# Seven-product second product for three token groups, shorter scale and root chains, and a new written-out order

## The chip, the cores and the metric

The kernel runs on one core of a Trainium2 chip. The metric is the device time of one execution in microseconds (us). Three executions of the kernel before took 697.19, 697.19 and 699.59 us, median 697.19 us. The profile that is read below is of one more execution, which took 698.44 us.

## The reference

Three stages follow one another on 2304 tokens (4 batches of 576). The matrices are large enough that most of the arithmetic lies in the last stage.

```python
# 1: attention, 8 heads of 64; heads 0-3 see the last 32 positions,
#    heads 4-7 every fourth of the last 128
scores = where(mask[h], q @ k.T / 8, -1e9)
x = softmax(scores) @ v                       # 2304 x 512
# 2: first MLP, d_ff 1024
h = x @ moe_w_in
solu = h * softmax(h)
ln = (solu - mean(solu)) / sqrt(var(solu) + 1e-6) * g_ln
y = ln @ moe_w_out                            # 2304 x 512
# 3: second MLP, d_ff 2048
h = y @ moe2_w_in
g = maximum(h, 0) + log1p(exp(-abs(h)))       # softplus
out = g @ moe2_w_out                          # 2304 x 512
```

Inputs and outputs are float32; the `moe` weights (first MLP and second) arrive as 64-bit floats.

## The kernel before, in words

**Precision.** Almost every product runs in float16 on TensorE (PE). Each operand is scaled by a power of two and split into a high and a low float16 half, and the product is three matmuls that add up in PSUM: high by high, high by low, low by high. A *split* is therefore two instructions per operand: the high half (VectorE, called DVE here, or ScalarE, called ACT), then the low half as a residue (DVE, `scalar_tensor_tensor` or `tensor_tensor`).

**Scales.** For each of the ten weight pieces (`w1i`, `w1o`, four quarters of `w2i` and of `w2o`) and for q, k and v of each batch, ACT squares the pieces and leaves one column of sums per piece. PE multiplies these columns by a matrix of ones (a float32 matmul, line L552), which gives every partition the column totals; DVE then adds the columns (`tensor_reduce`, L738 or L660) and makes the scale out of the sum in four one-column instructions (`scale_of`, L580: floor, two shifts, reciprocal, times a power of two). The weights cannot be split before that.

**Root.** For each of 18 token tiles of 128, the layer norm needs one over the root of the variance. `m1` (L1186) computes it on DVE in one-column instructions: an integer first guess (shift, then subtract from a constant) and three Newton steps of two instructions, then a last multiplication.

**Groups.** The second MLP works on groups of 256 tokens, numbered 0 to 8. Groups 0 to 4 go through `mlp2`: for each of eight blocks of 256 hidden features, the hidden product, softplus on ACT, a split of the result `g`, and the second product (`outp`): for two halves of the tokens and two halves of the features three matmuls of 128x512, so 12 a block. Groups 5, 6 and groups 7, 8 are *twins*: `mlp2_twin` takes two groups at once and does the first product of each feature quarter (a `unit`) in seven half-size products `P1` to `P7` instead of eight (L1550). For that `twin_weights` makes sums and differences of the weights, `y_twin` those of y, and DVE adds up the seven results (`U`, `C`). The second product of the twins is the same `outp` as above, 12 matmuls of 128x512 a block:

```python
for ti in range(2):
    for ff in range(2):
        f = 2 * fh + ff
        for x, (a, w) in enumerate(((0, 0), (0, 1), (1, 0))):
            mm(po.t[:, ti], gb.t[:, a, ff, ti*128:(ti+1)*128], w2o[qd][:, w, f, :], ...)
```

At the end of a group two instructions bring the PSUM accumulators into `osb` and two transfers write 256 rows of the output.

**Order.** Every instruction belongs to a named operation with the operations that it comes after and the buffers that it uses. Nothing is scheduled at run time: the table `ORDER` (L190) lists the operations one by one, `SLOTS` the buffer that each takes, and the engines get their instructions in that order; all transfers are issued by SyncE (SP) in that order too. Negative entries of `ORDER` are *fills*: matmuls of the identity `eye` by itself, 128x512 in bfloat16, into a free PSUM bank, whose result nobody reads. There are 142 of them, all in the first third of the program.

Of the kernel before, what the change touches and what calls it, by code (L numbers as in the profile page):

```python
# [1749 lines left out]
```

## Time and profile before

| | |
|---|---|
| executions, us | 697.19, 697.19, 699.59 (median 697.19) |
| the profiled execution, us | 698.44 |
| its span, first to last instruction, us | 696.5 |
| PE busy, us (share) | 675.2 (97%) |
| DVE busy, us (share) | 556.0 (80%) |
| ACT busy, us (share) | 480.9 (69%) |
| TensorE clock granted, mean | 0.988 of full |
| HBM read, written, MB | 54.53, 4.72 |

The profiled execution lasted 1.9 us longer than its span (698.44 against 696.5), which is what lies before its first and behind its last instruction. "Busy" is the time in which an engine had at least one instruction in flight; a busy PE may also be running fills. The chain of waits is the chain of work that ended last, followed back from the last instruction; 69% of the span on it is PE, 12% DVE and 10% DMA.

### The profile page before, as it was taken

The page shows a single profiled execution, that of the slowest core. Times are in us where ns is not written, and L with a number is a line of the kernel's source. Part 1 is how long each engine was busy: PE and PEld are TensorE (multiplying, and loading weights), DVE is VectorE, ACT ScalarE, POOL GpSimd, SP SyncE. Part 2 cuts the span into 40 slices and gives each one's busy share as a digit, 9 for nine tenths or more (in the row PEclk, how much of TensorE's full clock was granted, in tenths as well). Part 3 has the DMA queues.
Part 4 walks back from the last instruction along what each step waited for, and adds up shares of the span by engine and source line. Part 5 has one row for each costly group of instructions (what it writes and reads, how often), then busy time and mean ns, then how long its engine had stood idle before and what let it go on. Part 6 is the DMA issues. An engine that isn't in the chain of part 4 may idle for free.

```text
span 696.5 us, 14184 instructions
## 1 busy us (share of the span) xinstructions
PE 675.2 (97%) x5223; PEld 463.9 (67%) x5223; DVE 556.0 (80%) x1619; ACT 480.9 (69%) x1015; POOL 3.5 (1%) x22
## 2 busy tenths in 40 slices
PE   7999699999999999999999999999999999999997
PEld 4665547766765588688667668666776668676653
DVE  4999999999999968788889899887887768544233
ACT  4889998999998776987799797976364632322312
POOL 2000000000000000000000000000000000000000
PEclk9999689999999999999999999999999999999999
DMA  9889987669876558989887887652012110000001
GB/s 266 247 233 259 225 225 193 162 170 188 184 147 164 146 176 185 200 162 157 158 152 153 153 162 136 116 113 43 1 31 62 31 31 1 1 32 31 1 1 60
DMA packets 186773, 89.80 MB, mean 129 GB/s; under 512 B 157000, under 2 KB 174416, under 8 KB 186704
## 3 DMA queue, kind: packets, MB, share of 16 engines
q1 hardware_dynamic: 186704, 88.90, 56.4%
q8 instruction: 41, 0.67, 0.4%
q14 instruction: 28, 0.23, 0.1%
HBM read 54.53 MB, written 4.72 MB: 85 GB/s over the span
## 4 chain that ended last, share of the span: by engine, by line
PE 69%; DVE 12%; DMA 10%; ACT 4%; issue 3%; SPq 1%; ACTq 0%; DVEq 0%
PE ps_w L552 31%; PE bank L552 26%; PE bank L1550 11%; DMA xd<-x 2%; DVE E L543 2%; DMA E<-in_v_dram 2%; DMA qT<-qk 1%; DMA pT<-p 1%; DVE W L543 1%; PE bank L558 1%; DVE s L1122 1%; DMA W<-in_moe_w_out_dram 1%; ACT E L534 1%; DMA rv<-in_v_dram 1%; DMA rq<-in_q_dram 1%
## 5 line engine op out<-in xcount | busy, mean ns | idle before, releaser
L552 PE MATMUL ps_w<-W,g 128*128 128x512 f16 x864 | 194.3, 379 | 0.0
L552 PEld LDWEIGHTS <-W 128*128 128x128 f16 x1824 | 176.5, 98 | 23.3 <-DMA lnT<-hl 0.7
L552 PEld LDWEIGHTS <-g 128*128 128x128 f16 x864 | 83.6, 98 | 91.4
L552 PE MATMUL bank<-y,W 128*128 128x256 f16 x960 | 109.9, 273 | 0.0
L552 PE MATMUL ps_w<-W,xr 128*128 128x512 f16 x432 | 99.5, 382 | 1.0 <-ACT xr L534 1.0
L552 PE MATMUL bank<-lnT,W 128*128 128x256 f16 x864 | 98.7, 273 | 0.2 <-DMA lnT<-hl 0.2
L552 PEld LDWEIGHTS <-xr 128*128 128x128 f16 x432 | 42.1, 99 | 46.9 <-ACT xr L534 1.5
L543 DVE SCALAR_TENSOR_TENSOR g<-r,KR,g 128x512 f16<-128x512 f32 x68 | 50.3, 744 | 15.2 <-ACT g L534 14.2
L1718 ACT ACT_TABLE_LOAD x43 | 55.2, 1283 | 0.7
L1550 PEld LDWEIGHTS <-W 128*128 128x128 f16 x480 | 47.0, 98 | 8.4
L534 ACT ACTIVATE E<-E 128x768 f32<-128x768 f32 (+3 forms) x51 | 37.9, 744 | 15.7 <-DVE E L543 8.8
L534 ACT ACTIVATE s<-s 96x128 f32<-96x128 f32 (+3 forms) x144 | 43.5, 374 | 2.4 <-DVE st L538 1.2
L1122 DVE CUSTOM_DVE_ANT_0 s<-bank,band,bsc 96x128 f32<-96x128 f32 (+3 forms) x144 | 38.9, 324 | 3.9 <-PE bank L552 3.6
L534 ACT ACTIVATE r<-bank,invC 128x512 f32<-128x512 f32 x40 | 27.2, 685 | 16.4 <-PE bank L552 15.5
L534 ACT ACTIVATE r<-r,invT 128x512 f32<-128x512 f32 x21 | 14.6, 714 | 32.5 <-DVE r L546 32.4
L534 ACT ACTIVATE xf<-bank,rs 80x64 f32<-80x64 f32 (+1 forms) x128 | 29.3, 314 | 7.2 <-DVE rs L549 4.8
L552 PE MATMUL ps_w<-eye 128*128 128x512 bf16 x108 | 31.4, 407 | 0.7 <-DVE e L543 0.7
L534 ACT ACTIVATE g<-r,KR 128x512 f16<-128x512 f32 x35 | 24.9, 715 | 6.6 <-PE ps_w L552 6.3
L552 PEld LDWEIGHTS <-pT 128*96 128x96 f16 (+3 forms) x432 | 23.1, 123 | 6.9 <-issue 1.5
L543 DVE SCALAR_TENSOR_TENSOR E<-E 128x512 int32<-128x512 int32 x40 | 27.1, 683 | 0.1
L552 PEld LDWEIGHTS <-eye 128*128 128x128 bf16 (+2 forms) x162 | 16.5, 111 | 15.8 <-POOL eye L611 4.0
L534 ACT ACTIVATE hl<-e,st 128x1024 f16<-128x1024 f32 x18 | 22.3, 1242 | 5.4 <-DMA lnT<-hl 3.2
(295 smaller groups left out, 1102.9 us busy)
## 6 DMA issues: line engine op xcount, KB each, us to landing
E<-in_moe_w_in_dram SPq DMA_DIRECT2D x17, 512.0 KB, 4.8
E<-in_moe_w_out_dram SPq DMA_DIRECT2D x17, 512.0 KB, 4.1
out_dram<-osb SPq DMA_DIRECT2D x18, 256.0 KB, 2.4
W<-in_moe_w_in_dram SPq DMA_DIRECT2D x7, 512.0 KB, 5.7
W<-in_moe_w_out_dram SPq DMA_DIRECT2D x7, 512.0 KB, 6.2
E<-in_v_dram SPq DMA_DIRECT2D x9, 384.0 KB, 4.0
E<-in_q_dram SPq DMA_DIRECT2D x9, 384.0 KB, 3.4
E<-in_k_dram SPq DMA_DIRECT2D x9, 384.0 KB, 3.4
```

Source lines behind the costliest of these rows:

```text
L534: pin(nc.scalar.activation(out=out, in_=in_, func=func, **kw))
L543: pin(nc.vector.scalar_tensor_tensor(out=out, in0=in0, scalar=s, in1=in1, op0=op0, op1=op1, **kw))
L552: pin(nc.tensor.matmul(out, l, r, start=start, stop=stop))
L558: pin(nc.tensor.transpose(out, in_, eye32[:in_.shape[0], :in_.shape[0]]))
L1122: pin(nc.vector.tensor_tensor_reduce(out=sv()[:rows, h, :nk], in0=sb.t[:rows, h, :nk], in1=band[:rows, 48 - m:48 - m + nk], scale=sc[:rows ...
L1550: pin(nc.tensor.matmul(ps.t[:, ff, :], at(w, cc, ff), yo.t[:, v, cc, :], start=start, stop=cc == 1 and x == 2, skip_group_check=True,))
L1718: pin(nc.scalar.preload_act_table_set(TABLES[tab]))
```

## The change

**Second product of groups 6, 7 and 8** (`OTW`). The blocks of these three groups are kept back until their `g` is there and then go through `out_seven`: the 256 tokens by 256 features of `g` and the 256 features by 512 columns of the weights are cut into two halves each way, and seven products of quarter matrices replace eight. One block is then 7 products of 3 matmuls of 128x256, so 21 matmuls instead of 12 of 128x512. What DVE and ACT have to do for that:

- `twin_out_weights`, once for each of the eight blocks of weights, shared by the three groups: two sums that rebuild the float32 weight (128x512), four differences (128x256), two splits (128x512).
- in `step`, for each block of each group: the ordinary split, now for 384 of 512 columns; four sums and differences of 128x128 (`so..1`, `.3`, `.2`, `.4`, each on the result of the one before), and a second split, 128x512 (`ho`, `lo`).
- `end`, for each group: eight instructions of 128x256 that scale the seven results and add them up, instead of two of 128x512.

The new buffers lie in memory that the attention, the first MLP and the y stage have left; the third weight sum of `twin_weights` moves into a part of `w2i` itself, behind the last plain hidden product.

**Chains.** The totals are now added up on PE (one float32 matmul per column, all into one PSUM column), the `tensor_reduce` is gone, and the reciprocal and its multiplication have become one integer instruction, so that `scale_of` is three instructions. The root's chain has seven instructions ahead of the last multiplication instead of nine (shift and subtraction in one, two of the Newton steps replaced by one step of higher order).

**Order.** `ORDER` and `SLOTS` are new throughout. The transfers on SP stand in the same order up to the 79th; fills are 132 instead of 142.

```diff
+    OTW = (6, 7, 8)
...
-        65, 66, 247, 248, 278, 277, 0, 13, -2, -2, -2, 250, 252, 2943, 3, 2945, 14, 67, 69, -2, -2, 280, 254, 281,
...
+        63, 231, -2, 234, 232, -2, 236, 3146, 64, 235, -2, -2, 238, 239, 262, 261, 264, 265, 250, 0, 1, 13, 3, 4,
...
-            (TINY, lambda e: ts(sc, ss() if callable(ss) else ss, 2.0 ** -80, op0=ALU.max)),
+            (dve_cost(0, x=1), lambda e: ts(sc, ss(), 2.0 ** -80, op0=ALU.max), [], uses),
             (TINY, lambda e: ts(i, i, 24, 23, ALU.logical_shift_right, ALU.logical_shift_left)),
-            (TINY, lambda e: recip(inv, sc)),
-            (TINY, lambda e: ts(inv, inv, 2.0 ** -50)),
+            (TINY, lambda e: ts(inv.bitcast(INT32), i, -1.0, float((254 - 50) << 23), ALU.mult, ALU.add)),
...
-        m = P.op(f"{name}m", pe_cost(0.15), lambda e: mm(pb.t[:, 0:n], ones, am[:, 0:n], True, True), after=squares, uses=[pb])
+        def total(e):
+            for i in cols:
+                mm(pb.t[:, 0:1], ones, am[:, i:i + 1], i == cols[0], i == cols[-1])
...
-            (TINY, lambda e: pin(nc.vector.tensor_reduce(out=t[:, 0:1], in_=pb.t[:, 0:n], axis=AXX, op=ALU.add)), [], [pb]),
-            *scale_of(inv, sc, t[:, 0:1]),
+            *scale_of(inv, sc, lambda: pb.t[:, 0:1], [pb]),
...
-            lambda e: ts(i32(9), i32(7), 1, op0=ALU.logical_shift_right),
-            lambda e: ts(i32(9), i32(9), -1.0, float(0x5F3759DF - 2 ** 31), ALU.mult, ALU.add),
+            lambda e: ts(i32(9), i32(7), -0.5, float(0x5F3759DF - 2 ** 31), ALU.mult, ALU.add),
             lambda e: stt(col(10), col(9), col(9), col(7), ALU.mult, ALU.mult),
-            lambda e: stt(col(9), col(10), 3.0, col(9), ALU.subtract, ALU.mult),
+            lambda e: stt(col(8), col(10), 10.0 / 3.0, col(10), ALU.subtract, ALU.mult),
+            lambda e: stt(col(9), col(8), 5.0, col(9), ALU.add, ALU.mult),
             lambda e: stt(col(10), col(9), col(9), col(7), ALU.mult, ALU.mult),
-            lambda e: stt(col(9), col(10), 12.0, col(9), ALU.subtract, ALU.mult),
-            lambda e: stt(col(10), col(9), col(9), col(7), ALU.mult, ALU.mult),
-            lambda e: stt(col(10), col(10), 768.0, col(9), ALU.subtract, ALU.mult),
+            lambda e: stt(col(10), col(10), 64.0 / 3.0, col(9), ALU.subtract, ALU.mult),
...
+    def twin_out_weights(p):
...
+            P.op(
+                f"to{p}f{i}", dve_cost(512), lambda e, i=i: tt(F[i].t, wt[:, 0, f + i, :], wt[:, 1, f + i, :], ALU.add),
+                after=[*w2_d[p // 2][1]], uses=[F[i]],
+            ) for i in range(2)
...
+        t1 = P.op(f"to{p}t1", dve_cost(256), lambda e: tt(F[0].t[:, lo], F[0].t[:, hi], F[0].t[:, lo], ALU.subtract), after=[o[0]], uses=[F[0]])
...
+    def out_seven(n):
...
+        def step(p, k, rb, gb, split):
...
+            cost = dve_cost(128)
+            s1 = P.op(f"so{m}.1", cost, lambda e: tt(a22(), a21(), a22(), ALU.add), after=split, uses=[rb])
+            s3 = P.op(f"so{m}.3", cost, lambda e: tt(a21(), a11(), a21(), ALU.subtract), after=[s1], uses=[rb])
+            s2 = P.op(f"so{m}.2", cost, lambda e: tt(a11(), a22(), a11(), ALU.subtract), after=[s3], uses=[rb])
+            s4 = P.op(f"so{m}.4", cost, lambda e: tt(a12(), a12(), a11(), ALU.subtract), after=[s2], uses=[rb])
+            h2 = P.op(f"ho{m}", either(512, ptr=1), lambda e: scaled(e, g2.t[:, 0], rb.t, KR[:, cq]), after=[s4], uses=[rb, g2])
...
+                for q, gt, ff, t, b, start in which:
+                    start = start and new
+                    for x, (a, w) in enumerate(((0, 0), (0, 1), (1, 0))):
+                        pin(nc.tensor.matmul(
+                            mi[q](), gt.t[:, a, ff, 128 - 128 * t:256 - 128 * t], b(w), start=start and x == 0, stop=x == 2, skip_group_check=True,
+                        ))
...
+            parts = {
+                "a": ((1, gb, 0, 0, plain(0, 0), True),),
+                "b": ((5, g2, 1, 1, summed(0), True), (6, g2, 0, 0, summed(3), False), (7, g2, 0, 1, summed(1), True)),
+                "c": ((2, gb, 1, 0, plain(1, 0), False), (4, gb, 1, 1, summed(2), False), (3, g2, 1, 0, plain(1, 1), True)),
+            }
+            ready = {"a": split, "b": [h2, l2], "c": [*split, h2, l2]}
...
+        def end():
...
+            u2 = plus("u2", lambda: ub.t[:, hi], 6, lambda: ub.t[:, lo], [m1_, *all_ops["b"]], [*both, ub])
...
+            c12 = plus("c12", lambda: o1.t[:, hi], 3, lambda: o1.t[:, hi], [u4, *all_ops["c"]], [*both, o1])
+            c21 = plus("c21", lambda: o2.t[:, lo], 4, lambda: o2.t[:, lo], [u3, c22, *all_ops["c"]], [*both, o2], niD[:, 0:1])
```

**The order at two places.** The first is DVE at the scale of the first weight, `w1i` (`s1i` holds that scale, `bank` is PSUM, `W` and `E` hold raw weights, `xr` and `s` belong to the attention). Before:

```order
L1013 TENSOR_REDUCE s_112<-bank_139 96x4
L546 TENSOR_TENSOR xr<-bank_138,xr 128x2x72
L540 TENSOR_SCALAR W<-E 128x512
L738 TENSOR_REDUCE tmp_90<-bank_137 128x1
L538 TENSOR_SCALAR s1i<-tmp_90 128x1
L540 TENSOR_SCALAR s1i<-s1i 128x1
L549 RECIPROCAL s1i<-s1i 128x1
L538 TENSOR_SCALAR s1i<-s1i 128x1
L543 SCALAR_TENSOR_TENSOR W<-E,W 128x512
L538 TENSOR_SCALAR W<-W,s1i 128x512
```

And with the change:

```order
L562 TENSOR_TENSOR xr<-bank_138,xr 128x2x72
L1034 TENSOR_REDUCE s_113<-bank_139 96x4
L556 TENSOR_SCALAR W<-E 128x512
L554 TENSOR_SCALAR s1i<-bank_138 128x1
L556 TENSOR_SCALAR s1i<-s1i 128x1 x2
L559 SCALAR_TENSOR_TENSOR W<-E,W 128x512
L554 TENSOR_SCALAR W<-W,s1i 128x512
```

Five one-column instructions have become three, and the first of them reads PSUM itself. On PE one matmul `bank<-amw,ones 128x8` has become eight of 128x1.

The second place is the end of DVE's program (`g` and `s`, `v` hold splits, `r`, `e` and `W` softplus results, `p` a sum of the last group, `osb` output rows). Before:

```order
L546 TENSOR_TENSOR r_126<-bank_137,osb_135 128x512
L543 SCALAR_TENSOR_TENSOR g_131<-hl,KR,g_131 128x512
L538 TENSOR_SCALAR g_130<-r_126,KR 128x512
L538 TENSOR_SCALAR osb_133<-ps_w_141,iD 128x512
L538 TENSOR_SCALAR g_129<-r_127,KR 128x512
L543 SCALAR_TENSOR_TENSOR g_129<-r_127,KR,g_129 128x512
L543 SCALAR_TENSOR_TENSOR g_130<-r_126,KR,g_130 128x512
L538 TENSOR_SCALAR osb_133<-ps_w_140,iD 128x512
```

And with the change, of which these are 12 consecutive rows shortly before the last sums of `end`:

```order
L562 TENSOR_TENSOR W<-W 128x128 x3
L559 SCALAR_TENSOR_TENSOR s_113<-e_118,KR,s_113 128x512
L559 SCALAR_TENSOR_TENSOR s_114<-W,KR,s_114 128x512
L559 SCALAR_TENSOR_TENSOR g_132<-r_127,KR,g_132 128x384
L562 TENSOR_TENSOR r_127<-r_127 128x128 x2
L559 SCALAR_TENSOR_TENSOR g_131<-r_126,KR,g_131 128x384
L562 TENSOR_TENSOR r_127<-r_127 128x128
L562 TENSOR_TENSOR r_126<-r_126 128x128
L562 TENSOR_TENSOR r_127<-r_127 128x128
L562 TENSOR_TENSOR r_126<-r_126 128x128 x3
L559 SCALAR_TENSOR_TENSOR v_112<-r_127,KR,v_112 128x512
L559 SCALAR_TENSOR_TENSOR s_114<-r_126,KR,s_114 128x512
```

Where a block had one or two DVE instructions, it now has a split, four small sums in a chain and a second split, one block's between another's. From the first twin product (`P1` of groups 5, 6) to the end, DVE has 395 instructions with the change and had 214.

## Rows read from the trace of the kernel before

**Rows 1.** The page: busy time, and the span in 40 slices (tenths).
```profile
PE 675.2 (97%) x5223; PEld 463.9 (67%) x5223; DVE 556.0 (80%) x1619; ACT 480.9 (69%) x1015; POOL 3.5 (1%) x22
...
PE   7999699999999999999999999999999999999997
...
DVE  4999999999999968788889899887887768544233
```
**Rows 2.** Busy us by stretch: length, PE, PEld, DVE, ACT, POOL; clock, DMA share, GB/s.
```profile
0.00:100.00 100.00, 87.85 (x640) 56.19 (x641) 87.15 (x235) 82.12 (x244) 3.54 (x22) 0.91 0.93 248
100.00:237.00 137.00, 134.87 (x1050) 91.52 (x1048) 133.81 (x414) 122.43 (x275) 0.00 (x0) 1.00 0.72 169
237.00:493.90 256.90, 254.38 (x2183) 183.77 (x2182) 217.57 (x756) 204.64 (x393) 0.00 (x0) 1.00 0.72 144
493.90:692.00 198.10, 198.06 (x1357) 132.46 (x1354) 116.76 (x217) 71.03 (x103) 0.00 (x0) 1.00 0.09 22
```
**Rows 3.** Chain of waits, 56 to 76 us: start, us, what.
```profile
56.91 7.85 DMA W<-in_moe_w_out_dram
...
67.56 0.07 DVE tmp L738
...
69.74 5.82 DMA E<-in_v_dram
```
**Rows 4.** Chain of waits, the twin stage: y products (128x256), second products (128x512).
```profile
480.81 13.10 PE bank L552 x120
...
547.38 15.54 PE ps_w L552 x72
```
**Rows 5.** DVE in order of time, twin stage: start, us, instruction.
```profile
565.51 0.69 DVE L546 TENSOR_TENSOR W<-kT,W 128x512 f16<-128x512 f32 x1 [2.77 <-ACT W L534]
566.12 0.68 DVE L546 TENSOR_TENSOR v<-W 128x512 f32<-128x512 f16 x1
566.72 0.69 DVE L546 TENSOR_TENSOR W<-xd,W 128x512 f16<-128x512 f32 x1
```
**Rows 6.** DVE in order of time, 132 to 135 us.
```profile
133.78 0.34 DVE L546 TENSOR_TENSOR xr<-bank,xr 128x192 f16<-128x192 f32 x1
134.04 0.74 DVE L543 SCALAR_TENSOR_TENSOR qk<-rk,bsc,qk 128x512 f16<-128x512 f32 x1
134.70 0.74 DVE L543 SCALAR_TENSOR_TENSOR W<-W,s2i 128x512 f16<-128x512 f32 x1
```
**Rows 7.** DVE in order of time: the scale chain of w1i.
```profile
32.98 0.17 DVE L738 TENSOR_REDUCE tmp<-bank 128x1 f32<-128x8 f32 x1
33.18 0.15 DVE L538 TENSOR_SCALAR s1i<-tmp 128x1 f32<-128x1 f32 x1
33.37 0.15 DVE L540 TENSOR_SCALAR s1i<-s1i 128x1 int32<-128x1 int32 x1
33.56 0.16 DVE L549 RECIPROCAL s1i<-s1i 128x1 f32<-128x1 f32 x1
```
**Rows 8.** DVE in order of time: one-column instructions of different chains, then a high half.
```profile
122.27 0.15 DVE L538 TENSOR_SCALAR s2i<-s2i 128x1 f32<-128x1 f32 x1
122.34 0.15 DVE L543 SCALAR_TENSOR_TENSOR bsc<-bsc,s1i 128x1 f32<-128x1 f32 x1
122.41 0.15 DVE L543 SCALAR_TENSOR_TENSOR st<-st 128x1 f32<-128x1 f32 x1
122.48 0.48 DVE L538 TENSOR_SCALAR W<-W,s2i 128x512 f16<-128x512 f32 x1
122.87 0.21 DVE L538 TENSOR_SCALAR st<-st,bsc 128x1 f32<-128x1 f32 x1
```
**Rows 9.** Groups by line: line engine op out<-in shapes xcount, busy us, mean ns, idle before.
```profile
L534 ACT ACTIVATE g<-r,KR 128x512 f16<-128x512 f32 x35 | 24.9, 715 | 6.6 <-PE ps_w L552 6.3
...
L552 PE MATMUL ps_w<-eye 128*128 128x512 bf16 x108 | 31.4, 407 | 0.7 <-DVE e L543 0.7
...
L552 PE MATMUL bank<-eye 128*128 128x512 bf16 x34 | 10.8, 421 | 4.9 <-POOL eye L611 4.0 <-ACT qk L534 0.9
...
L552 PE MATMUL bank<-amw,ones 128*128 128x4 f32 x16 | 2.9, 252 | 0.8 <-ACT W L534 0.6 <-ACT E L534 0.2
```
**Rows 10.** PE in order of time: the totals of w1i (one float32 matmul, two passes).
```profile
32.66 0.28 PE L552 MATMUL bank<-amw,ones 128*128 128x8 f32 x2
```
**Rows 11.** All engines in order of time, the end of the program.
```profile
682.73 9.23 PE L552 MATMUL ps_w<-W,g 128*128 128x512 f16 x42
...
692.04 0.69 ACT L534 ACTIVATE osb<-ps_w,iD 128x512 f32<-128x512 f32 x1 [8.95 <-issue]
692.76 0.75 DVE L538 TENSOR_SCALAR osb<-ps_w,iD 128x512 f32<-128x512 f32 x1 [6.69 <-ACT osb L534]
```

More of the change, by code (lines that the diff above doesn't have):

```diff
@@ L423 @@
     iD = mem([128, 1], FP32, "iD")
+    niD = mem([128, 1], FP32, "niD")
     KR0 = mem([128, NQ], FP32, "KR0")
@@ L1355, in y_stage @@
             y_ops[j] += [yh, yl]
+    plain_h = [[] for _ in range(NQ)]
     def mlp2(j):
@@ L1519, in y_twin, with products, plus @@
         split("t4", b21, [t4])
         return ops
+    def out_seven(n):
+        if not to_done:
+            for p in range(NP):
+                twin_out_weights(p)
+        pa, pb = Buf(ps_w), Buf(ps_w)
+        mi = (None, lambda: pa.t[:, 0, 0:256], lambda: pa.t[:, 0, 256:512], lambda: pb.t[:, 1, 0:256], lambda: pb.t[:, 0, 0:256],
+              lambda: pa.t[:, 1, 0:256], lambda: pa.t[:, 1, 256:512], lambda: pb.t[:, 0, 256:512])
+        firsts = {}
+        all_ops = {x: [] for x in "abc"}
+        def step(p, k, rb, gb, split):
+            wt, f = w2o[p // 2], (2 * p) % 4
+            tb, td = to_done[p]
+            g2 = Buf(gq_pool)
+            c = p // 2
+            cq = slice(c, c + 1)
+            a11, a12, a21, a22 = (lambda ff=ff, t=t: rb.t[:, ff, 128 * t:128 * t + 128] for t in (1, 0) for ff in range(2))
+            m = f"{n}.{p}"
+            cost = dve_cost(128)
[4 more added lines that the diff above has]
+            h2 = P.op(f"ho{m}", either(512, ptr=1), lambda e: scaled(e, g2.t[:, 0], rb.t, KR[:, cq]), after=[s4], uses=[rb, g2])
+            l2 = P.op(
+                f"lo{m}", dve_cost(512, x=1), lambda e: stt(g2.t[:, 1], rb.t, KR[:, cq], g2.t[:, 0], ALU.mult, ALU.subtract), after=[h2], uses=[rb, g2],
+            )
+            plain = lambda ff, dh: (lambda w: wt[:, w, f + ff, 256 * dh:256 * dh + 256])
+            summed = lambda i: (lambda w: tb.t[w][:, 256 * i:256 * i + 256])
+            def products(which, new):
+                for q, gt, ff, t, b, start in which:
[4 more added lines that the diff above has]
+                        ))
+            now = {x: x not in firsts for x in "abc"}
+            parts = {
[4 more added lines that the diff above has]
+            ready = {"a": split, "b": [h2, l2], "c": [*split, h2, l2]}
+            for x, which in parts.items():
+                used = [pa, pb, *([gb] if x != "b" else []), *([g2] if x != "a" else []), *([tb] if x != "a" else [])]
+                o = P.op(
+                    f"o{x}{m}", pe_cost(0.109 * 3 * len(which)), lambda e, which=which, new=now[x]: products(which, new), cols=0.768 * len(which),
+                    after=[*ready[x], *w2_d[c][1], *(td if x != "a" else []), *firsts.values()], uses=used,
+                )
+                firsts.setdefault(x, o)
+                all_ops[x].append(o)
+        def end():
+            o1, o2, ub = Buf(osb_pool), Buf(osb_pool), Buf(ue_pool)
+            lo, hi = slice(0, 256), slice(256, 512)
+            cost = dve_cost(256, x=1)
+            d = iD[:, 0:1]
+            def plus(name, out, q, in1, after, uses, by=d):
+                return P.op(f"oe{n}{name}", cost, lambda e: stt(out(), mi[q](), by, in1(), ALU.mult, ALU.add), after=after, uses=uses)
+            both = [pa, pb]
+            m1_ = P.op(f"oe{n}m1", either(256, ptr=1, psum=1), lambda e: scaled(e, ub.t[:, lo], mi[1](), d), after=all_ops["a"], uses=[*both, ub])
+            u2 = plus("u2", lambda: ub.t[:, hi], 6, lambda: ub.t[:, lo], [m1_, *all_ops["b"]], [*both, ub])
+            u3 = plus("u3", lambda: o2.t[:, lo], 7, lambda: ub.t[:, hi], [u2], [*both, ub, o2])
+            u4 = plus("u4", lambda: o1.t[:, hi], 5, lambda: ub.t[:, hi], [u2], [*both, ub, o1])
+            c11 = plus("c11", lambda: o1.t[:, lo], 2, lambda: ub.t[:, lo], [m1_, *all_ops["c"]], [*both, ub, o1])
+            c22 = plus("c22", lambda: o2.t[:, hi], 5, lambda: o2.t[:, lo], [u3], [*both, o2])
+            c12 = plus("c12", lambda: o1.t[:, hi], 3, lambda: o1.t[:, hi], [u4, *all_ops["c"]], [*both, o1])
+            c21 = plus("c21", lambda: o2.t[:, lo], 4, lambda: o2.t[:, lo], [u3, c22, *all_ops["c"]], [*both, o2], niD[:, 0:1])
+            for ti, (ob, w) in enumerate(((o2, [c21, c22]), (o1, [c11, c12]))):
+                r0 = n * GRP + ti * 128
+                P.op(f"out{n}.{ti}", dma_cost(0.5, 2.0), lambda e, r0=r0, ob=ob: dma(out[r0:r0 + 128, :], ob.t), after=w, uses=[ob], mv=moving(128, 2048))
+        return step, end
@@ L1522, in mlp2_twin, with split @@
     def mlp2_twin(j, ops):
-        po = [Buf(ps_w), Buf(ps_w)]
+        po = [None if j + th in OTW else Buf(ps_w) for th in range(2)]
         o_prev = [None, None]
+        later = [[], []]
+        seven = [out_seven(j + th) if j + th in OTW else None for th in range(2)]
+        def split(name, rb, gb, cq, after, c0=0):
+            part = lambda t: t.rearrange("p f c -> p (f c)")[:, c0:]
+            gh = P.op(f"gh{name}", either(512 - c0, ptr=1), lambda e: scaled(e, part(gb.t[:, 0]), part(rb.t), KR[:, cq]), after=after, uses=[rb, gb])
+            gl = P.op(
+                f"gl{name}", dve_cost(512 - c0, x=1), lambda e: stt(part(gb.t[:, 1]), part(rb.t), KR[:, cq], part(gb.t[:, 0]), ALU.mult, ALU.subtract),
+                after=[gh], uses=[rb, gb],
+            )
+            return [gh, gl]
@@ L1578, in unit @@
                 )
-                gh = P.op(f"gh{n}.{k}", either(512, ptr=1), lambda e, rb=rb, gb=gb, cq=cq: scaled(e, gb.t[:, 0], rb.t, KR[:, cq]), after=[sp], uses=[rb, gb])
-                gl = P.op(
-                    f"gl{n}.{k}", dve_cost(512, x=1),
-                    lambda e, rb=rb, gb=gb, cq=cq: stt(gb.t[:, 1], rb.t, KR[:, cq], gb.t[:, 0], ALU.mult, ALU.subtract), after=[gh], uses=[rb, gb],
-                )
+                if seven[th] is not None:
+                    later[th].append((f"{n}.{k}", 2 * qd + fh, k, rb, cq, sp))
+                    continue
+                gb = Buf(g_pool)
+                gh, gl = split(f"{n}.{k}", rb, gb, cq, [sp])
                 first = o_prev[th] is None
@@ L1598, in mlp2_twin @@
         for th in range(2):
+            if seven[th] is not None:
+                step, end = seven[th]
+                for name, p, k, rb, cq, sp in later[th]:
+                    gb = Buf(go_pool)
+                    step(p, k, rb, gb, split(name, rb, gb, cq, [sp], 128))
+                end()
+                continue
             for ti in range(2):
@@ L1682 @@
     opd = lambda t: t.bitcast(FP16).rearrange("p (a f c) -> p a f c", a=2, f=2)
+    y_all = [o for o in P.ops if o.name[:2] in ("ya", "yb")]
+    yf_all = [u for x in yf_pool.bufs for u in x.users]
+    xr_mem = xr.rearrange("p k a t -> p (k a t)").bitcast(FP32)
+    ln_mem = ln_pool.slots[0][0].rearrange("p a t -> p (a t)").bitcast(FP32)
+    cut = lambda t, i: t[:, 512 * i:512 * i + 512]
     for i in range(7):
         yo_pool.add(opd(slots[i]), opens=att, until=7, place=places[i])
-    for i in range(7, 10):
-        yo_pool.add(opd(slots[i]), opens=att, since=7, place=places[i])
     for i in range(4):
-        yo_pool.add(opd(y_mem[i // 2][:, 512 * (i % 2):512 * (i % 2) + 512]), opens=plain_y, since=7)
+        yo_pool.add(opd(cut(y_mem[i // 2], i % 2)), opens=plain_y, since=7)
+    for t in (cut(xr_mem, 4), cut(xr_mem, 5), cut(WF, 6)):
+        yo_pool.add(opd(t), opens=m1_all, since=7)
     for i in range(10, 14):
@@ L1694 @@
         u_pool.add(t, opens=early_osb)
-    parts = lambda t: t.bitcast(FP16).rearrange("p (k a f c) -> p k a f c", k=4, a=2, f=2)
+    parts = lambda t: t.bitcast(FP16).rearrange("p (k a f c) -> p k a f c", k=3, a=2, f=2)
     for i in range(2):
-        tw_pool.add(parts(E[:, 2048 * i:2048 * (i + 1)]), opens=att, until=2)
+        tw_pool.add(parts(E[:, 1536 * i:1536 * (i + 1)]), opens=att, until=2)
     for i in range(2):
-        tw_pool.add(parts(WF[:, 2048 * i:2048 * (i + 1)]), opens=m1_all, since=2)
+        tw_pool.add(parts(WF[:, 1536 * i:1536 * (i + 1)]), opens=m1_all, since=2)
     e_mem = e_pool.slots[0][0]
-    for t in (e_mem, hl_mem):
-        for i in range(2):
-            r_pool.add(two(t[:, 512 * i:512 * (i + 1)]), opens=m1_all)
+    for i in (6, 7):
+        r_pool.add(two(cut(E, i)), opens=att)
+    for t in (cut(e_mem, 0), cut(e_mem, 1), cut(hl_mem, 0), cut(hl_mem, 1), cut(WF, 7)):
+        r_pool.add(two(t), opens=m1_all)
+    both = lambda a, b: (a.bitcast(FP16), b.bitcast(FP16))
+    for i in range(2):
+        t2_pool.add(both(cut(xr_mem, 2 * i), cut(xr_mem, 2 * i + 1)), opens=m1_all)
+    for i in range(4):
+        t2_pool.add(both(cut(WF, 8 + 2 * i), cut(WF, 9 + 2 * i)), opens=y_all)
+    for i in range(2):
+        t2_pool.add(both(cut(ln_mem, 2 * i), cut(ln_mem, 2 * i + 1)), opens=y_all)
+    for i in (10, 11, 12):
+        gq_pool.add(slots[i].bitcast(FP16).rearrange("p (a f c) -> p a f c", a=2, f=2), opens=yf_all)
+    ue_pool.add(slots[13], opens=yf_all)
+    g_all = [u for x in g_pool.bufs for u in x.users]
+    for x in g_pool.slots:
+        go_pool.add(x[0], opens=g_all, place=x[4])
     for p in (qk_pool, qT_pool, kT_pool, pT_pool, xd_pool):
```

79 lines of the change are left out of this document (52 added, 27 removed), and 366 rows, old and new, of tables (ORDER, SLOTS).

## The prediction, made before the changed kernel was run

> **What bounds the kernel now.** I read the page first: PE is busy for 675.2 of 696.5 us and in nearly every slice [rows 1]; DVE falls from full in the first half to a third at the end. But a busy PE need not be doing the kernel's work: the fills alone are 31.4 + 10.8 = 42.2 us of it [rows 9]. So I split the span by what limits each part [rows 2]. Up to 237 us all the fills are run; between 100 and 237 DVE is busy for 133.81 of 137 us, and together with transfers on the chain of waits (7.85 and 5.82 us in one stretch [rows 3]) it sets the pace; PE fills its gaps. From 237 to 493.9, where the first twin product starts, PE lacks 256.90 - 254.38 = 2.5 us. From 493.9 to 692 PE is busy for 198.06 of 198.10 us, and here its work is all useful, while DVE is needed for 116.76 (59%). The end is 4.5 us of eviction and transfer behind the last matmul. So a matmul saved in the last stage counts in full as long as DVE keeps up, a matmul in the first stage hardly counts, and a DVE instruction counts in the first stage and not in the last. The change moves work from PE to DVE in the last stage and takes a little from DVE in the first.
>
> **Second product, PE.** 72 matmuls of 128x512 take 15.54 us, 0.2158 each; 120 of 128x256, each with its own weight load as the new ones have, take 13.10 us, 0.1092 each [rows 4]. A block falls from 12 x 0.2158 = 2.590 us to 21 x 0.1092 = 2.293 us. Three groups of eight blocks: 24 x 0.297 = **-7.1 us**, from the stage that PE fills.
>
> **What DVE must do for it.** Prices are distances from one start to the next in a full queue, not recorded durations. A 128x512 `tensor_tensor` costs 0.605 us (565.51 to 566.72 for two [rows 5]), a residue 0.66 and a 128x192 sum 0.26 [rows 6], a high half 0.39 [rows 8]. No row has the new 128x128; between 192 and 512 columns a column costs (0.605 - 0.26)/320 = 0.00108 us, so I take 0.19 for 128, 0.33 for 256, 0.38 for a 128x256 sum that scales too, and a residue of 384 columns is 0.14 cheaper than one of 512. Added: 32 instructions of 128x512 for the weights (19.4), 32 of 128x256 (10.6), 96 of 128x128 (18.2), 24 residues (15.8), 21 sums at the ends of groups (8.0): 72.0 us. Taken away: 24 residues shortened (3.4), six high halves fewer by the order (2.3), four evictions (2.6), two `U` sums gone to ACT (1.2): 9.5. Net +62.5, all behind the first twin product because the new buffers lie in memory that frees only there. DVE then needs 116.8 + 62.5 = 179.3 us where PE needs 198.1 - 7.1 = 191.0.
>
> That leaves 11.7 us, and not all of it. In a chain whose instructions stand one behind another, starts are 0.19 us apart (33.18, 33.37, 33.56 [rows 7]) where unrelated ones are 0.07 apart [rows 8]: 0.12 us of waiting. The order has 43 of the new 128x128 sums directly behind the one they need: 5.2 us. What is left is 6.5 us, 3.4% of the stage. Between 100 and 237 us DVE ran with 2.3% idle [rows 2], so it can be that full, but there PE paid with fills. ACT, at 71.03 us [rows 2], gains 39 instructions, 28 us at 0.715 each [rows 9], and stays at about half. With PE in program order, a block that is late holds everything behind it. I put these stalls at **+4.0 us**, between 0 (the order hides all) and 16.6 (rival B).
>
> [...]
>
> **Start.** Up to the last weight scale the change takes 47 one-column instructions from DVE: two from each of ten weight scales, seven from two batches, two from each of nine root tiles, two elsewhere. Among unrelated work one costs 0.07 us [rows 8], so 3.3 us; alone in its chain 0.19 [rows 7], so 8.9. PE gets 46 more small totals. Today's takes 0.28 us in two passes [rows 10], but a pass alone shows 0.25 [rows 9], so the second began 0.03 after the first; at 0.06 a total that is 2.7 us, in a stage with 42.2 us of fills to take it. Eight totals in a row lengthen w1i's chain by 7 x 0.06 = 0.4 us, which the two instructions saved behind them give back. The lower bound is thus nothing, where a transfer is the last to come [rows 3]. Of the 3.3 us I take **-2.5**, since DVE is nearly but not always the last. The ten fills fewer count nothing by themselves.
>
> **Middle and end.** The middle is searched anew, with 2.5 us of PE waits to lose or to double: **0**. Behind the last matmul stood 0.69 and 0.75 us of eviction, one after the other [rows 11]; now three sums at 0.38, 1.1 us, while four others lie beside the last two PE operations (18 matmuls, 2.0 us). Between -0.3 and +1.6 if none is hidden: **0**.
>
> **Sum.** -7.1 + 4.0 - 2.5 = -5.6 us. The profiled execution lasted 698.44 us, so 692.8 in its terms; it was 1.25 us above the median of the three, so **691.6 us** (0.8% less).
>
> **The rivals.** About 0.5%, 3.5 us, is what a measurement of this kernel can tell from no change; so faster is below 693.7, slower above 700.7.
>
> *A, the order hides all.* No stalls, and the saved DVE instructions are paid nearer to the chain price, 6 us: -7.1 - 6 = -13.1, 684. For it: PE lost 0.04 us in 198 before [rows 2]. Against it: then DVE had 81 us to spare.
>
> *B, DVE becomes the bound of the last stage.* Each block is a chain (split, four sums, high half on ACT, residue). If instructions cost their recorded length, 0.08 us more for each of the 181 that the stage has gained (14.5), if half of the 24 blocks leave DVE waiting for ACT's 0.715 [rows 9] (8.6), and the 43 waits stand (5.2), DVE takes 207.6 us, 16.6 more than PE: -7.1 - 2.5 + 16.6 = +7.0, 704. It decides for slower from 24.8 us of uncovered waits (191.0 + 9.6 + 3.5 - 179.3), for no gain from 21.3. For it: 93% to 97% on an engine that waits in order. Against it: the residues and sums of neighbouring blocks stand between each other in the order, and DVE was 98% busy in the first stage. [...]
>
> *C, the start gives it back.* Behind the 79th transfer the order is new. One more wait of the size of those on the chain, 5.82 us [rows 3], takes -5.6 to about 0: 697. For it: the start is a race of transfers, DVE and ACT, in which a piece a few places later is a wait. Against it: the first 79 lie where the DMA share was highest (0.93 [rows 2]), and they stay.
>
> That the change doesn't do what it says can be left out: the order shows 504 matmuls of 128x256 in place of 288 of 128x512.
>
> **Chances.** Forecast (PE still the bound of the last stage, a few us of stalls) 0.48, A 0.14, B 0.16, C 0.22. Faster: nine tenths of the forecast, all of A and a trace of C, 0.59. Within 0.5%: the rest of the forecast and most of C, 0.24. Slower: B and a trace of C, 0.17. The range goes from A's 684 to B's 704 and leaves out about one in five beyond; the forecast's own is 687 to 696, from stalls of 0 to 8.
>
> **What would show it.** Second products at 0.109 us a matmul, 21 to a block: the first step. DVE between 175 and 185 us busy from the first twin product to the last matmul, with PE idle of some 4 us, put down to DVE residues: the second; idle of 10 us or more there, with DVE near 97%, is B. The first twin product about 2.5 us earlier for the same PE work ahead of it, with fills and idle of PE before it down by about that: the start; a new DMA wait there on the chain is C. The prediction would be wrong in its grounds, whatever the total, if PE were never idle in the last stage, or if a 128x256 matmul took more than 0.115 us.

## The result: slower by 0.9%

| | before | after |
|---|---|---|
| median, us | 697.56 (697.19 to 699.59, 4 runs) | 704.86 (703.71 to 705.59, 4 runs) |
| ratio, 95% interval | | 1.0094 (1.0075 to 1.0113) |
| span of the profiled execution, us | 696.5 | 703.8 |
| last matmul begins, us | 691.58 | 699.16 |

A second measurement, beside the experiments, gave 1.0098 (1.0067 to 1.0130). The forecast, 691.6, missed in sign; 704.86 lies just above its range.

The page after the change: busy time and the 40 slices of PE, DVE and PE's granted clock. It answers to [rows 1].

```profile
PE 678.9 (96%) x5521; PEld 496.3 (71%) x5521; DVE 614.6 (87%) x1752; ACT 501.2 (71%) x1039; POOL 3.5 (1%) x22
...
PE   7999899999999999999999989999999999999996
...
DVE  3899899999999778788888978878988999999985
...
PEclk9999789999999999999999999999999999999998
```

PE is busy for longer than before (675.2), though the second product took matmul time from it. DVE is now nearly full to the end (87% of the span, before 80%). Busy time by stretch, as in [rows 2] (length; PE, PEld, DVE, ACT, POOL; clock, DMA share, GB/s); the first twin product now starts at 507.6 us and the last matmul ends at 699.4:

```profile
0.00:100.00 100.00, 92.09 (x660) 61.10 (x661) 81.27 (x209) 80.64 (x239) 3.53 (x22) 0.91 0.91 240
100.00:237.00 137.00, 134.75 (x1084) 95.11 (x1083) 130.57 (x389) 126.49 (x278) 0.00 (x0) 1.00 0.74 166
237.00:507.60 270.60, 266.31 (x2257) 190.91 (x2256) 225.70 (x764) 207.93 (x385) 0.00 (x0) 1.00 0.73 143
507.60:699.40 191.80, 185.53 (x1525) 149.15 (x1523) 175.79 (x391) 86.09 (x138) 0.00 (x0) 1.00 0.08 20
```

In the first 100 us DVE does 6 us less than before and PE is busy for 4 us more. In the last stretch DVE works 175.79 us, as forecast (175 to 185), and PE stands idle for 6.3 us, which it did not do before.

**Where the time went.** For one reckoning over the whole span, take the start of a matmul block and subtract the matmul work that the order puts ahead of it, every operation at the same price in all kernels, fills and totals left out. What remains is all that was lost up to there: idle time, fills, totals and half clock. That is a granted clock of 0.50 of full, as from 698.2 to 699.2 us (after), where the 128x256 matmuls stand 0.213 us apart in place of 0.109. In us, one execution each; the last columns are experiments below:

| lost up to | before | after | totals alone (e0) | one total (e1) | e5 |
|---|---|---|---|---|---|
| first layer-norm tile (48 to 51 us) | 29.9 | 32.2 | 31.4 | 29.0 | 28.9 |
| tile 4 (132 to 138) | 58.5 | 62.2 | 61.5 | 55.3 | 56.0 |
| tile 9 (337 to 353) | 65.7 | 70.6 | 70.3 | 60.2 | 60.5 |
| last tile (515 to 532) | 68.3 | 75.3 | 73.1 | 65.1 | 64.6 |
| last matmul | 68.3 | 83.1 | 73.1 | 72.9 | 68.8 |

The work itself fell by 7.2 us (the seven products). Against it stand 7.0 us more lost before the last tile and 7.8 us more behind it: -7.2 + 7.0 + 7.8 = +7.6, what the last matmul shows. Two places, then. A second profiled execution of the changed kernel (e7 below), reckoned in the same way, differs from the column "after" by -1.6, -3.8, -1.3, +0.2 and +0.8 us from the first row to the last: the last two rows can be relied on to about 1 us, the rows above them only to some 4.

**The first: the totals.** A float32 matmul of a total stands in the trace as two matmul records (20 for the ten totals of the weights, before), called passes here, and each has a weight load (PEld) of its own (96 of both, after). Groups by line and shape, after (busy us, mean ns of one; then idle before):

```profile
L568 PE MATMUL ps_w<-eye 128*128 128x512 bf16 x110 | 30.8, 399 | 1.2 <-DVE e L559 1.2
L568 PEld LDWEIGHTS bank<-amw,ones 128*128 128x128 f32 x96 | 12.8, 203 | 1.3 <-DVE xr L562 0.3
L568 PE MATMUL bank<-amw,ones 128*128 128x1 f32 x96 | 12.5, 253 | 0.0
L568 PE MATMUL bank<-eye 128*128 128x512 bf16 x22 | 7.3, 442 | 4.0 <-POOL eye L626 4.0
```

The totals of the weights went from 20 passes (16 of them, with 2.9 us, are in [rows 9]; the other four are those of `w1i` and `w1o`) to 96 passes and 12.5 us, and those of the batches from 8 passes to 24. All engines in order of time, after, around the totals of `w1i` (last column: idle before, and who ended it):

```profile
32.97 2.13 PE L568 MATMUL bank<-amw,ones 128*128 128x1 f32 x16
...
35.14 0.16 DVE L554 TENSOR_SCALAR s1i<-bank 128x1 f32<-128x1 f32 x1 [1.44 <-PE bank L568]
35.34 0.34 DVE L556 TENSOR_SCALAR s1i<-s1i 128x1 int32<-128x1 int32 x2
...
35.71 1.34 ACT L550 ACTIVATE W<-W,s1i 128x512 f16<-128x512 f32 x2 [0.99 <-DVE s1i L556]
```

Before, two passes took 0.28 us [rows 10], and the scale was ready 1.25 us after the total began (32.66 [rows 10] to 33.91, the end of the last step of its chain):

```profile
33.76 0.15 DVE L538 TENSOR_SCALAR s1i<-s1i 128x1 f32<-128x1 f32 x1
```

Now 16 passes take 2.13 us (with a pause of 0.28 from the second to the third), DVE stands still for 1.44 of them and ACT for 0.99, and the scale is ready after 2.71 us. The chain that lost two instructions became longer by 1.5 us. Later totals look like this, here with no fill within 2 us of them (PE alone):

```profile
241.02 0.95 PE L568 MATMUL bank<-amw,ones 128*128 128x1 f32 x8
```

From start to start these passes are 0.112 us apart, except the second, which begins 0.03 behind the first; ten of the 14 totals begin so, in the others the second comes 0.07 to 0.23 behind the first. The two passes of a total before show that first distance only, but what PE does next shows the other: behind the two passes at 32.66 [rows 10] it begins its next matmul at 32.80, 0.112 us after the second pass, and so or slower behind every total of the trace of before. Its attention also has float32 products in a row, eight passes with 96 columns loaded, 0.085 us apart. Both, before:

```profile
32.80 0.53 PE L558 MATMUL bank<-eye,rq 96*128 96x96 f32 x4
...
37.76 0.81 PE L552 MATMUL bank<-xd,pT 128*96 128x65 f32 x8
```

**The second: the last stage.** What PE waited for between 507.6 and 699.4 us (us in total, times, longest):

```profile
PE ps_w L1612 <- DVE osb L559: 3.5, 2, 2.3
PE ps_w L1612 <- ACT p L550: 0.8, 2, 0.6
PE bank L1696 <- DVE osb L562: 0.8, 1, 0.8
PE bank L1696 <- DVE r L562: 0.5, 1, 0.5
PE ps_w L1612 <- DVE v L559: 0.3, 1, 0.3
PE bank L1696 <- DVE e L562: 0.3, 1, 0.3
```

Over half of it, the 4.3 us of the two largest rows on `ps_w`, is the sums at the ends of groups, not the splits that the prediction looked at. The longest, in order of time:

```profile
693.19 1.15 PE L1612 MATMUL ps_w<-lnT,s 128*128 128x256 f16 x9
694.04 0.48 DVE L554 TENSOR_SCALAR p<-ps_w,iD 128x256 f32<-128x256 f32 x1 [0.81 <-PE ps_w L1612]
...
696.06 0.48 DVE L559 SCALAR_TENSOR_TENSOR osb<-ps_w,iD,p 128x256 f32<-128x256 f32 x1
696.59 0.49 PE L1612 MATMUL ps_w<-W,g 128*128 128x256 f16 x3 [2.25 <-DVE osb L559]
...
698.73 0.85 PE L1612 MATMUL ps_w<-W,v 128*128 128x256 f16 x3
```

The last two operations of PE (`oc8.6`, `oc8.7`: products 2, 4 and 3 of the last two blocks, 18 matmuls) stand behind five sums of DVE whose results they do not use. Three matmuls then take 0.49 us, a little later 0.85: the granted clock fell. Busy time by stretch there, the granted clock third from the end of a row:

```profile
680.00:694.00 14.00, 13.63 (x124) 11.73 (x123) 12.71 (x33) 7.34 (x12) 0.00 (x0) 1.00 0.00 1
694.10:696.60 2.50, 0.25 (x4) 0.07 (x2) 2.27 (x5) 0.00 (x0) 0.00 (x0) 1.00 0.00 0
696.60:699.60 3.00, 2.98 (x18) 2.02 (x17) 0.00 (x0) 0.00 (x0) 0.00 (x0) 0.68 0.00 0
```

The 16 distances from one start to the next that are longer than the usual 0.109 or 0.216 us behind the last tile (called gaps below, by what they are longer) add up to 7.7 us: 2.4 here, 0.7 at half clock behind it, 1.45 at 675.5 and 0.40 at 672.8 (the end of group 7), the rest between 0.2 and 0.7 each.

### The profile page after: what moved, and what is told of

It reads as the page before. It is cut to its first block, busy times and chain, and to the rows that moved or that the text cites. A ratio compares the mean times of both kernels' runs of the same rounds, so it can differ in the third digit from the quotient of the medians.

```text
span 703.8 us, 14956 instructions
## 1 busy us (share of the span) xinstructions
PE 678.9 (96%) x5521; PEld 496.3 (71%) x5521; DVE 614.6 (87%) x1752; ACT 501.2 (71%) x1039; POOL 3.5 (1%) x22
## 5 line engine op out<-in xcount | busy, mean ns | idle before, releaser
L568 PEld LDWEIGHTS <-W 128*128 128x128 f16 x1824 | 176.6, 98 | 24.1 <-DMA lnT<-hl 1.4
L568 PE MATMUL ps_w<-W,g 128*128 128x512 f16 x576 | 130.1, 379 | 0.0
L568 PEld LDWEIGHTS <-g 128*128 128x128 f16 x576 | 55.5, 98 | 60.8
L568 PEld LDWEIGHTS <-xr 128*128 128x128 f16 x432 | 42.2, 100 | 46.7 <-issue 2.5
L1696 PEld LDWEIGHTS <-W 128*128 128x128 f16 x528 | 51.7, 98 | 8.4 <-issue 1.6
L559 DVE SCALAR_TENSOR_TENSOR g<-r,KR,g 128x512 f16<-128x512 f32 (+1 forms) x55 | 39.4, 717 | 3.4 <-ACT g L550 3.1
L550 ACT ACTIVATE r<-bank,invC 128x512 f32<-128x512 f32 x40 | 27.2, 683 | 11.5 <-PE bank L568 9.2
L550 ACT ACTIVATE g<-r,KR 128x512 f16<-128x512 f32 (+1 forms) x39 | 26.6, 686 | 6.8 <-PE ps_w L568 5.2
L1612 PE MATMUL ps_w<-W,g 128*128 128x256 f16 x180 | 26.1, 274 | 3.8 <-DVE osb L559 3.5
L550 ACT ACTIVATE xf<-bank,rs 96x64 f32<-96x64 f32 (+1 forms) x112 | 25.6, 312 | 5.7 <-DVE st L559 2.6
L568 PE MATMUL bank<-v,pT 128*96 128x65 f16 (+3 forms) x432 | 23.5, 206 | 3.9 <-DMA pT<-p 3.9
```

What stands on the lines that cost most here:

```text
L550: pin(nc.scalar.activation(out=out, in_=in_, func=func, **kw))
L559: pin(nc.vector.scalar_tensor_tensor(out=out, in0=in0, scalar=s, in1=in1, op0=op0, op1=op1, **kw))
L568: pin(nc.tensor.matmul(out, l, r, start=start, stop=stop))
L1612: pin(nc.tensor.matmul(mi[q](), gt.t[:, a, ff, 128 - 128 * t:256 - 128 * t], b(w), start=start and x == 0, stop=x == 2, skip_group_check=True,
L1696: pin(nc.tensor.matmul(ps.t[:, ff, :], at(w, cc, ff), yo.t[:, v, cc, :], start=start, stop=cc == 1 and x == 2, skip_group_check=True,))
```

## The experiments

Theory 1: the totals cost PE 0.224 us a matmul (two passes of 0.112) and lengthen the scale chains. Rival 2: the new order of the start lost the time, through waits for transfers. Theory 3: the wait at the end is a matter of shared PSUM tiles. Rival 4: DVE is simply late. The edits are shown in short form. The ratio in brackets is to the kernel before, with its 95% interval.

**e0, the totals alone, put into the kernel before.** Same order; the reduction stays, over one column.

```diff
- mm(pb.t[:, 0:n], ones, am[:, 0:n], True, True)
+ for i in range(n):
+     mm(pb.t[:, 0:1], ones, am[:, i:i + 1], i == 0, i == n - 1)
```

> The kernel before, with one thing of the change alone: each total of squares is taken by several one-column float32 matmuls that add up in PSUM, 46 more in all, in place of one; the DVE reduction stays, over one column. Theory 1 (a total costs PE two passes of 0.112 us each, not 0.06): 46 x 0.224 = 10.3 us more on PE, of which the ten totals from 95 us on, 6.0 us, stand where no fill can take them. Slower by 6 us, between 4 and 9. Rival (the price of the prediction, 0.06 a total, taken by fills): slower by 0 to 1.5 us.

Measured: 701.52 us (1.0064, 1.0040 to 1.0088), 4.7 us slower. That is inside the range of theory 1 and far outside the rival's. In the table 3.0 of its 4.8 us are lost by tile 4 (one execution each), in the stretch where nearly all the fills stand. So fills do not hide the totals: both kernels run all 142 fills, each in its place in PE's order, so that a total comes on top of them, and the weights cannot be split before the scale is there. In order of time, PE, DVE and ACT behind the totals of `w1i`:

```profile
32.67 1.84 PE L552 MATMUL bank<-amw,ones 128*128 128x1 f32 x16
...
34.55 0.16 DVE L738 TENSOR_REDUCE tmp<-bank 128x1 f32<-128x1 f32 x1 [1.59 <-PE bank L552]
...
34.94 0.49 ACT L534 ACTIVATE qT<-bank 128x384 f32<-128x384 f32 x1 [1.40 <-PE bank L558]
```

The total begins where it did before (32.67 against 32.66 [rows 10]) and everything behind it is 1.6 us late. Of the 10.3 us that 46 matmuls cost, 4.7 showed. The pages show what took the rest: PE is busy for 11.1 us more (686.3 against 675.2) in a span that is 4.8 us longer (701.3 against 696.5), so 6.3 us came out of PE's idle time, 4.9 of them between the first layer-norm tile and tile 4.

**e1, one total again, in the changed kernel.** The reduction is folded into the first step of the scale chain, so the order is unchanged. **e2, two products exchange their places in PSUM. e3, both.**

```diff
  # e1
- for i in cols:
-     mm(pb.t[:, 0:1], ones, am[:, i:i + 1], i == cols[0], i == cols[-1])
+ mm(pb.t[:, 0:n], ones, am[:, 0:n], True, True)
  # e2: product 2 to pb, product 7 to pa
- 2: pa.t[:, 0, 256:512]    7: pb.t[:, 0, 256:512]
+ 2: pb.t[:, 0, 256:512]    7: pa.t[:, 0, 256:512]
```

> The changed kernel with each total taken by one matmul again, and a DVE reduction folded into the first step of the scale chain; same order. Theory 1: faster than the changed kernel by 6 us, between 4 and 9, so about 699 and close to the kernel before. Rival 2 (the new order of the start and of the attention is what lost the time ahead of the twin products, through waits for transfers): within 1 us of the changed kernel's 704.9.

> The changed kernel with the partial products 2 and 7 of the second product exchanging their places in PSUM, so that products 2, 3 and 4 have one PSUM tile to themselves and 1, 5, 6 and 7 the other. Theory 3 (PE waits for the sums of a group only because both write and read parts of one tile, not because it needs them): the wait of 2.4 us ahead of the last two operations goes, with the halved clock behind it (0.7 us) and the 0.4 us at 672.8: faster than the changed kernel by 3 us, between 1.5 and 3.5. Rival 4 (DVE is late in any case, and the wait moves to the sums behind the last matmul): faster by 0.5 us at most.

> The changed kernel with one matmul for each total and with the exchanged places in PSUM. If theories 1 and 3 hold and are independent, the gains add up: faster than the changed kernel by 9 us, between 6 and 12, so about 696, and faster than the kernel before by 0 to 4 us. If the order's waits are the cause (rivals 2 and 4), within 1.5 us of 704.9.

*e1:* 694.42 us (0.9961, 0.9941 to 0.9982), 10.4 us faster than the changed kernel (9.3 by the two ratios), more than the 4 to 9 that theory 1 gave, and a little faster than the kernel before. This one step decides the sign. The same place in order of time:

```profile
32.88 0.39 PE L568 MATMUL bank<-amw,ones 128*128 128x8 f32 x2 [0.24 <-DVE s L1036]
...
33.31 0.17 DVE L597 TENSOR_REDUCE tmp<-bank 128x1 f32<-128x8 f32 x1
33.51 0.15 DVE L554 TENSOR_SCALAR s1i<-tmp 128x1 f32<-128x1 f32 x1
33.69 0.34 DVE L556 TENSOR_SCALAR s1i<-s1i 128x1 int32<-128x1 int32 x2
...
34.10 1.33 ACT L550 ACTIVATE W<-W,s1i 128x512 f16<-128x512 f32 x2
```

Rival 2 falls: the new order, with one total, loses 65.1 us up to the last tile where the old one loses 68.3. Behind that tile nothing changed: the same gaps, 7.7 us.

*e2:* 703.76 us (1.0110, 1.0070 to 1.0151): no gain that can be told by the time, less than the 1.5 to 3.5 of theory 3. In its profile the wait at the end is gone and the gaps behind the last tile add up to 5.8 us in place of 7.7; from e1 to e3 they fall just so, from 7.7 to 5.8. *e3:* 692.07 us (0.9930, 0.9904 to 0.9956), 2.4 us below e1, with intervals that overlap a little. The profile of e3 shows why it is not 3.1: the wait at the end is gone and the sums lie beside the last matmuls, but the one at the end of group 7 has grown. In order of time:

```profile
663.70 0.75 DVE L559 SCALAR_TENSOR_TENSOR v<-r,KR,v 128x512 f16<-128x512 f32 x1 [2.28 <-ACT v L550]
...
665.08 1.27 DVE L559 SCALAR_TENSOR_TENSOR osb<-ps_w,iD,p 128x256 f32<-128x256 f32 x3
666.27 0.87 DVE L559 SCALAR_TENSOR_TENSOR osb<-ps_w,iD,osb 128x256 f32<-128x256 f32 x2
666.80 0.22 PEld L1614 LDWEIGHTS <-g 128*128 128x128 f16 x3 [2.24 <-DVE osb L559]
666.80 0.50 PE L1614 MATMUL ps_w<-W,g 128*128 128x256 f16 x3 [1.96 <-DVE osb L559]
667.14 1.69 PE L1614 MATMUL ps_w<-xr,v 128*128 128x256 f16 x9
```

PE waits 1.96 us, and then runs at half clock until 670.9 (0.60 in the mean of that stretch):

```profile
664.90:666.80 1.90, 0.00 (x0) 0.00 (x1) 1.86 (x6) 0.00 (x0) 0.00 (x0) 1.00 0.00 0
666.80:670.90 4.10, 4.10 (x23) 3.10 (x24) 4.00 (x11) 2.12 (x4) 0.00 (x0) 0.60 0.33 128
```

So theory 3 held for its place, and rival 4 was half right: a wait came back elsewhere. What made it: the residue `lo8.1` (663.70, `v<-r,KR,v`) had waited for its high half on ACT, and the sums of group 7 stood behind it on DVE.

**e4, the shorter chains alone, in the kernel before**, with one total; the places of the dropped instructions stay empty.

```diff
- recip(inv, sc)
- ts(inv, inv, 2.0 ** -50)
+ ts(inv.bitcast(INT32), i, -1.0, float((254 - 50) << 23), ALU.mult, ALU.add)
...
```

> The kernel before in its own order, with the shorter chains of the change alone: the reciprocal and the scaling of a weight scale become one integer instruction, the root has two instructions fewer in each of 18 tiles, two copies per batch and three of four invT go; totals and the second product as before, their places in the order stay empty. The prediction's step for the start: DVE saves 36 + 10 + 3 + 3 = 52 one-column instructions at 0.07 to 0.19 us, most of them where DVE or its chains are the last to come: faster than the kernel before by 2.5 us, between 0.5 and 5. Rival (a transfer or ACT is the last to come there): within 0.5 us.

Measured: 695.86 us (0.9979, 0.9956 to 1.0003): 1.2 us faster in the median, 3.0 in the profiled execution, no change not excluded. It agrees with the prediction's -2.5 and with half of it.

**e5, e3 with the sums of group 7 first**, and **e6, e5 with two products of the middle put earlier.** In names of operations in place of the numbers of `ORDER` (`lo` is a residue, `so` a small sum, `oe` a sum at the end of a group, `QK` scores, `PV` a weighted sum, `o` an output product):

```diff
  # e5, DVE
- gl7.0.1 so8.0.1 so8.0.3 lo8.1 so8.0.2 oe7u2 oe7u3 oe7u4 oe7c11 oe7c22 ...
+ gl7.0.1 so8.0.1 so8.0.3 oe7u2 oe7u3 oe7u4 oe7c22 lo8.1 so8.0.2 oe7c11 ...
  # e6, PE as well
- QK24.0 PV22.1 o3.5 QK24.1 PV23.0 o3.6
+ o3.5 QK24.0 PV22.1 QK24.1 o3.6 PV23.0
```

> The changed kernel with one total and the exchanged places in PSUM, and in addition the residue lo8.1 and one sum so8.0.2 moved behind four sums of group 7 (u2, u3, u4, c22) on DVE. Theory 5: these sums hold PE up for 2.1 us, with 20 matmuls at half clock behind it (1.9 us), only because lo8.1 stands ahead of them and waits for ACT: faster than the version without the move by 4 us, so about 688. Rival (DVE has too much to do there): the wait moves to the next product, less than 1 us.

> As the version with the sums first, and in the middle two output products (o3.5 and o3.6) put one place earlier on PE, ahead of the scores of pair 24 and of the weighted sum of pair 23. If waits for the transposes of pairs 23 and 24 (2.67 us and, in the version with one total, 1.7 and 1.1 us) cost their full length there, faster by another 2 to 3 us, about 685.5. Rival (the pairs then come later and the wait moves on): no difference.

> The changed kernel again, on the same chip as the three others, to compare with: 704.9 us, 1.0094 of the kernel before, between 1.0075 and 1.0113.

*e5:* 690.53 us (0.9897, 0.9867 to 0.9926), the fastest of all and 1% below the kernel before. Against e3 the ratios give 2.3 us, with intervals that overlap, and the medians 1.5, not 4: the half clock is gone (it had cost 16 gaps of 0.10, 1.6 us, not 20 and 1.9), but the wait of 2.1 us became six shorter ones of 0.1 to 0.6, 1.7 us in all, and one of 0.5 at 680.7 came back. The place in e5:

```profile
662.84 0.48 DVE L556 SCALAR_TENSOR_TENSOR p<-ps_w,iD,p 128x256 f32<-128x256 f32 x1 [1.67 <-ACT p L547]
...
664.54 0.74 DVE L556 SCALAR_TENSOR_TENSOR v<-r,KR,v 128x512 f16<-128x512 f32 x1
664.68 0.22 PEld L1611 LDWEIGHTS <-g 128*128 128x128 f16 x3 [0.38 <-DVE osb L556]
664.68 0.50 PE L1611 MATMUL ps_w<-W,g 128*128 128x256 f16 x3
```

*e6:* 690.72 us (0.9902, 0.9873 to 0.9931), no difference, as its rival had it, and not the 2 to 3 us that were expected. *e7*, the changed kernel beside them: 704.63 us (1.0098, 1.0067 to 1.0130).

**e8 and e9, which totals.** e1 gave back twice what e0 had cost. Is it the early totals, in the chains, or the late ones? The switch of e1 for `pre0`, `w1i`, `w1o`, `w2i0` alone (e8), and for all others (e9):

```diff
+ if name in ("w1i", "w1o", "w2i0"):
+     mm(pb.t[:, 0:n], ones, am[:, 0:n], True, True)
+     return
```

> The changed kernel with one matmul for each of the four totals up to 90 us (pre0, w1i, w1o, w2i0: 19 matmuls fewer), the ten later ones as in the change. With all fourteen it was 10.4 us faster. Theory 6 (each matmul saved counts its 0.224 us, fills or not): faster than the changed kernel by 19 x 0.224 = 4.3 us. Rival 7 (the early ones count through the scale chain, where DVE and ACT wait, and the later ones mostly fall into waits that PE has anyway, as in the kernel before): by 6 to 8 us.

> The changed kernel with one matmul for each of the ten totals from 98 us on (27 matmuls fewer), the first four as in the change. Theory 6: faster than the changed kernel by 27 x 0.224 = 6.0 us. Rival 7: by 2.5 to 4 us.

*e8:* 699.19 us (1.0034, 1.0011 to 1.0058), by the ratios 4.2 us faster than the changed kernel. *e9:* 697.11 us (0.9990, 0.9962 to 1.0018), 7.2 us faster. Each difference is known to some 2 us. That agrees with 4.3 and 6.0, a matmul at 0.224 us wherever it stands, and speaks against rival 7, clearly so for the late totals. Why did the same totals cost the kernel before only 4.7 us? There PE's idle time gave 6.3 us for them. In the changed order PE is busy for 11.5 us more with many totals than with one (678.9 against 667.4) and the span is 10.2 us longer (703.8 against 693.6), so idle time gave 1.3. Why the new order has less to give was not tried.

## Why the prediction was wrong, step by step

**Totals: the step that failed.** "PE gets 46 more small totals [...] at 0.06 a total that is 2.7 us, in a stage with 42.2 us of fills to take it." Both halves were wrong. A total costs 0.224 us, so 46 cost 10.3: two passes that stand 0.03 apart [rows 10] were read as the pitch of a series, but they show one distance, the only one in the series that is short. And the fills took nothing off: a fill stands in PE's order and is run like any other matmul, 142 times in e0 as before, and what can take a total is idle time of PE. Five of the ten later totals (at 167, 191, 220, 263 and 304 us, after) have no fill within 5 us anyway. "7 x 0.06 = 0.4 us, which the two instructions saved behind them give back" was +1.5 us. e1 prices the step at 9.3 to 10.4 us. The prediction took PE's share of a total from the total's own matmul rows alone; in the trace of before the next matmul behind a total, 0.112 us later, would have given the price, and a weight load stands beside each pass, recorded at 201 ns, which it left out.

At full clock the passes of the float32 products stand 0.112 us apart with 128 columns loaded (the totals), 0.085 with 96 and 0.072 with 80 (the last two in the attention, with 65 moving columns). Loads of 128 columns are recorded at 203 ns for the totals' float32 and 98 for the float16 `W`, after. At half clock the totals' passes are 0.213 us apart. The float32 transposes do not follow the columns loaded: they load 128, too, and stand 0.069 us apart, after:

```profile
66.74 0.44 PE L574 MATMUL bank<-eye,W 80*128 80x80 f32 x4
```

So the distance goes with the columns that a pass loads in the totals and in these products of the attention, and not in the transposes; that it is the load which holds PE up was not shown.

**Second product.** The step held: the new 128x256 matmuls stand 0.109 us apart, and the work fell by 7.2 us.

**Stalls of the last stage: mis-sized, and put in the wrong place.** +4.0 was taken, from 0 to 16.6; 7.7 us were measured. DVE's room was right (175.8 us busy in 191.8). About 5.0 us of it, with the half clock, were neither a full DVE nor a chain of splits, but the sums at the end of a group ahead of products that share their PSUM tiles. With the same work on DVE, e5 has 4.1 us. In the changed kernel the seven products thus brought nothing (-7.2 + 7.8 by the table), in e5 3.0 us (-7.2 + 4.2).

The last sum that PE waited for at 696.59 (`u4`, on product 5) reads the other half of its PSUM tile than the matmul behind it (product 2) writes. e2 and e3 show that places chosen by who reads when are enough: the wait at the end is gone, and the gaps are 5.8 us in place of 7.7.

**Start and middle.** -2.5 and 0 were taken. With one total the kernel has lost 3.2 us less than before up to the last tile (65.1 against 68.3), start and middle together. With many totals the middle was worse too (13.1 us lost from tile 4 to the last tile, 9.8 before and in e1). PE's largest waits for transfers between 100 us and the first twin product, after:

```profile
PE bank L568 <- DMA pT<-p: 3.9, 2, 2.7
PE bank L568 <- DMA lnT<-hl: 1.1, 1, 1.1
```

and before:

```profile
PE bank L552 <- DMA pT<-p: 1.0, 1, 1.0
PE bank L552 <- DMA qT<-qk: 0.9, 2, 0.5
```

**End.** 0 was taken, and 4.5 us behind the last matmul became 4.4.

**The sum, put together again:** -7.2 + 7.7 - 3.2 = -2.7, which is e1 (694.42 beside 696.83: -2.4), and the totals bring it to +7.3. The forecast's -5.6 differs from e1 mainly by the stalls.

**The rivals.** B has the time (704) and the wrong ground: DVE was not the bound, since e5 does the same work on it in 690.5. C has the place, the start, and the wrong mechanism. PE's waits for transfers between 100 us and the first twin product did grow, from 2.1 to 5.9 us, but with one total 4.9 of them are still there and the kernel is a little faster than before; what gave the start back were the instructions that the change itself added.
